# Retention attention with a gated linear unit: both weights through GpSimd's DMA queue, rounded to bfloat16 on the way

## The chip, the cores and the metric

The kernel runs on one core of a Trainium2 chip. The core has TensorE (PE; PEld is its weight load), VectorE (DVE), ScalarE (ACT) and GpSimd (POOL), which work at the same time on instructions of their own queues, each queue in its own order; SyncE (SP) does little but issue DMAs. ACT and POOL can issue DMAs too. Sixteen DMA engines move the data. The metric is the device time of one execution in microseconds (us); less is better.

## The reference

Inputs are float32: `q`, `k`, `v` of shape 8 x 8 x 576 x 64 (batch, heads, sequence, head width), two weights of 512 x 512 and the taps of a causal convolution, 5 x 512. The output is 8 x 576 x 512, float32.

```python
scores = (1 / np.sqrt(D)) * np.matmul(q, k.transpose(0, 1, 3, 2))
gamma = 1.0 - 2.0 ** (-5.0 - np.arange(H))
Dmat = np.where(rel >= 0, gamma[:, None, None] ** rel[None], 0.0)   # rel = query place - key place
x = np.matmul(scores * Dmat, v)          # 8 x 8 x 576 x 64, then heads side by side: 8 x 576 x 512
gate_pre = sum(conv_w[k] * xp[:, k:k + S, :] for k in range(5))   # xp: x with 4 zero rows ahead
gate = 1 / (1 + exp(-gate_pre))
out = (gate * (x @ w_val)) @ w_out
```

## The kernel before, in words

**Units.** The sequence of 576 is cut into units: for each of the 8 batches two full units of 256 rows, and two tail units, each with the last 64 rows of four batches. A unit's `q`, `k` and `v` are 512 KB each. The code counts units from 0; this text says first unit for unit 0. The work is pipelined over units: while one is multiplied, later ones are loaded, cast and transposed.

**Stages of a unit.** DMAs bring float32 tiles into slots `fk`, `fq`, `fv` (two slots each, of two halves; the first two units use larger slots, `big`, of which there are eleven). Casts make bfloat16 tiles `kb` and `qb` (L296, on POOL or ACT); `vb` is `v` times a decay, on POOL (L289). PE transposes `kb` and `qb` into PSUM, and ACT or DVE copies them to `kq`. PE makes scores from `kq`, DVE masks them into `p` (L385, L389). `update` multiplies keys by values, ACT copies the sum to `xf`, and POOL adds up the states carried along the sequence (`mid`, `run`, and their bfloat16 copies `s`, L520 to L531). `carried` and `values` make the attention's output in PSUM (`o`), DVE multiplies it by a decay into `xg` (L465). Then comes the gated unit: `conv` on PE and a sigmoid on ACT (`gate`, L576), `value` (`v<-xg,wvb`), the product of both on DVE (`z`, `zz`, L599), and `project` (`v<-wob,z`) with a copy to an output tile, which SP stores.

**What sets the order.** All of it is written out by hand, and each engine keeps the order in which its instructions are written. The first units are written one call after the other (L664 to L823), the others by a loop (L825). All matmuls are recorded at one line, L168.

**Loads and touches.** SP issues nearly all loads, in written order. A load waits until the slot's last reader is done. Where a load is given a `touch`, an engine first copies one element into the slot (L119), so that the DMA is issued only after that engine has come to this place in its own queue. A load can also be issued by ACT (`queue=nc.scalar`); it then stands in ACT's order. At most eight of these loads are under way: there are eight semaphores for them, used in turn, and each load waits for the landing of the one eight before it.

**The weights.** `w_val` and `w_out` are 1 MB each in float32. Both are loaded by SP in four DMAs of 256 KB. `w_val` (L150) goes through one slot of `fk` and one of `fq`, right behind the third unit's loads, and is cast to `wvb` by `prep_wv`: two casts on POOL (L265) and two on ACT (L267), which also swap the two halves of the partitions for `wvb[1]`. `w_out` (L160) goes through two slots of `big`, between the loads of the sixth and the seventh unit, and is cast to `wob` by `prep_wo` (L271), two casts on POOL, two on ACT. PE first needs `wvb` in `value(0, 0, 0)` (L755) and `wob` in the first `project` of the loop.

Of the kernel before, what the change touches and what calls it, by code (L numbers as in the profile page):

```python
# [13 lines left out]
F32 = mybir.dt.float32  # L14
# [7 lines left out]
def kernel(  # L22
# [29 lines left out]
    ldp = ctx.enter_context(tc.tile_pool(name="ld", bufs=2))  # L52
# [25 lines left out]
    half = (lo, hi)  # L78
    QUAD = ((0, 0), (1, 1), (0, 1), (1, 0))

    with tc.manual_schedule():
# [3 lines left out]
        def big():  # L85
            return ldp.tile([P, 2, DM], F32, name="big", bufs=11)
# [17 lines left out]
        def load_half(n, u, i, touch=None, queue=nc.sync):  # L104
            if u in whole:
                if i == 0:
                    load1(n, u, touch)
                return
            kind, b, c = units[u]
            if (n, u) not in loaded:  # L110
                t = ldp.tile([P, H, 2 * D], F32, name="f" + n)
                loaded[n, u] = [(t[:, g * HH:(g + 1) * HH], g * HH, HH) for g in range(2)]
                tiles[n, u] = t
            t = tiles[n, u]
            if kind == "tail" and i == 1:
                return
            hs = slice(i * HH, (i + 1) * HH)
            if touch:
                touch(t[0:1, i * HH, 0:1], lsc[0:1])  # L119
            if kind == "full":  # L120
                queue.dma_start(out=t[:, hs], in_=SRC[n][b, hs, c * W:(c + 1) * W, :].rearrange("h (p r) d -> p h (r d)", r=2))
            else:
                for g in range(GB):
                    nc.sync.dma_start(out=t[g * 32:(g + 1) * 32],
                                      in_=SRC[n][b + g, :, NC2 * W:S, :].rearrange("h (p r) d -> p h (r d)", r=2))

        def load(u):
            for n in "kqv":
                load1(n, u)
# [3 lines left out]
        cwn = consts.tile([KC * NP, 2, P], F32, name="cwn")  # L133
        taps = moe_conv_w.rearrange("k (o i) -> (k o) i", i=P)
        nc.scalar.dma_start(out=cwn, in_=taps.unsqueeze(1).to_broadcast([KC * NP, 2, P]))
        wvf = [None] * NP
        wvt = [None] * 2
        wof = [None] * NP
        load(1)


        def load_wv(o, touch=None):
            if wvf[o] is None:
                t = ldp.tile([P, 2, DM], F32, name=("fk", "fq")[o % 2])
                for i in range(2):
                    wvf[o % 2 + 2 * i] = t[:, i]
                wvt[o % 2] = t
            if touch:
                touch(wvf[o][0:1, 0:1], lsc[0:1])
            nc.sync.dma_start(out=wvf[o], in_=moe_w_val[o * P:(o + 1) * P, :])  # L150

        def load_wo(o, touch=None):
            if wof[o] is None:
                t = big()
                for c in range(2):
                    wof[o // 2 * 2 + c] = t[:, c]
            if touch:
                touch(wof[o][0:1, 0:1], lsc[0:1])
            blk = 2 * (o % 2) + o // 2
            nc.sync.dma_start(out=wof[o], in_=moe_w_out[blk * P:(blk + 1) * P, :])  # L160

        made = [0]
        BLOCK, PLACE = 127, 8
# [16 lines left out]
        lsc = small.tile([P, 1], F32, name="lsc")  # L180
# [64 lines left out]
        wvb = [consts.tile([P, 2, DM], BF16, name=f"wvb{e}") for e in range(2)]  # L245
        wob = consts.tile([P, NP, DM], BF16, name="wob")
        dg = consts.tile([P, NP, KC, 64], BF16, name="dg")

        def prep_conv():
# [9 lines left out]
                dg.rearrange("p o k j -> p k o j"),  # L259
                cw.rearrange("p (k o) -> p k o", o=NP).unsqueeze(3).to_broadcast([P, KC, NP, 64]),  # L260
                id2.unsqueeze(1).unsqueeze(1).to_broadcast([P, KC, NP, 64]), op=ALU.mult)

        def prep_wv():
            for i in range(2):
                nc.gpsimd.tensor_copy(wvb[0][:, i, :], wvt[0][:, i])  # L265
            for i in range(2):
                nc.scalar.copy(wvb[1][half[i]], wvt[1][half[1 - i]])  # L267

        def prep_wo(os, eng):
            for o in os:  # L270
                eng(wob[:, o, :], wof[o])  # L271

        def warm(n, cols=512, pool=None):
            z = (pool or ps_v).tile([P, 512], F32, name="s" if pool else "v")
# [24 lines left out]
        def cast1(n, u, eng=None):  # L299
            if u not in whole:  # L300
                for i in range(2):
                    cast_half(n, u, i, eng)
                return
            f = loaded[n, u][0][0]
            if n == "v":
                t = bfp.tile([P, H, 2, D], BF16, name="vb")
                nc.gpsimd.tensor_tensor(t.rearrange("p h r d -> p (h r) d"), f.rearrange("p h (r d) -> p (h r) d", r=2),
                                        gin[:, units[u][2]].rearrange("p h r -> p (h r)").unsqueeze(2)
                                        .to_broadcast([P, 2 * H, D]), op=ALU.mult)
            else:  # L310
# [344 lines left out]
        def gate_values(j, i, e):  # L655
            value(j, i, e)
            gated(j, i, e)

        table = small.tile([P, 1], F32, name="table")
        dve, act = nc.vector.tensor_copy, nc.scalar.copy  # L660

        pool = nc.gpsimd.tensor_copy
# [8 lines left out]
        prep_masks()  # L671
        cast1("v", 0)
        load(2)
        load_wv(0)
        load_wv(2)
        turn(0, ps_o, 0)
        take_part(0, 0, act)
        nc.scalar.activation(table, lsc, AF.Sigmoid)
# [23 lines left out]
        take_x(0, (1,))  # L702
        take_part(1, 1, dve)
        conv(0, 0)
        load_wv(1, act)
        load_wv(3)
        carried(1, 1, (0,))
        scores(1, 0)
        masks(1, 0)
        load_half("k", 3, 0, dve)  # L710
        scores(1, 1, pool=ps_a)
        masks(1, 1)
        load_half("k", 3, 1, dve)
        cast1("k", 2)
        update(1, own=True)
        cast1("q", 2, act)
        load_half("q", 3, 0, act)
# [18 lines left out]
        scores(2, 0)  # L736
        masks(2, 0)
        load_half("v", 3, 1, dve)
        prep_wv()
        cast1("k", 3)  # L740
        load_half("k", 4, 0)
        load_half("k", 4, 1)
# [8 lines left out]
        values(2, 1)  # L751
        take_x(2, (0,))
        load_half("v", 4, 0, dve)
        load_half("v", 4, 1)
        value(0, 0, 0)  # L755
        carried(2, 0)
        fence_last(2, dve)
# [2 lines left out]
        carried(2, 1)  # L760
        cast1("v", 3)
        cast1("q", 3, act)
        load_half("k", 5, 0, queue=nc.scalar)
        load_half("q", 5, 0, queue=nc.scalar)
        take_x(2, (1,))
        gated(0, 0, 1)
        load_half("k", 5, 1, dve)
# [11 lines left out]
        cast1("q", 4, act)  # L779
        conv(2, 0)  # L780
        cast1("v", 4)
        gate_values(1, 0, 1)
        load_wo(2, dve)
        load_wo(3)
        scores(3, 0)
        masks(3, 0)
        turn(4, ps_o, 0)
        take_part(4, 0, act)
        load_wo(0, dve)
        load_wo(1)  # L790
        turn(4, ps_o, 1)
        take_part(4, 1, act)
        scores(3, 1, pool=ps_a)
# [24 lines left out]
        load_half("k", 6, 1, dve)  # L818
        load_half("q", 6, 1)
        states(4, 1)  # L820
        prep_wo((0, 1), pool)
        cast_half("k", 6, 0)
        cast_half("q", 6, 0)  # L823

        for n in range(4, NU - 2):  # L825
            def bring(name, u, i, eng):
                if u < NU - 2:
                    load_half(name, u, i, eng)

            j, i = (HALVED, n - 4) if n < 6 else place[n - 2 - n % 2][0:1] + (n % 2,)  # L830
            rows = {4: [(0, 0), (0, 1), (1, 0)], 5: [(1, 1), (2, 0), (2, 1)]}.get(n, [(n - 3, 0), (n - 3, 1)])
            if NU - 2 <= n + 3 < NU:
                for name in "kqv":
                    load_half(name, n + 3, 0)
            scores(n, 1)
            masks(n, 1)
            conv(j, i)
            carried(n, 1)
            fence_last(n, dve)
            bring("k", n + 3, 0, act)  # L840
            scores(n + 1, 0, pool=ps_v)
            masks(n + 1, 0)
            update(n + 1, now=False)
            bring("q", n + 3, 0, act)
            if n == 4:
                prep_wo((2, 3), act)
            carried(n, 0)
            values(n, 0)
            values(n, 1)
            turns = ps_a.tile([P, 2, 2, 2, 2, P], BF16, name="a")  # L850
            turn_bank(n + 1, 1, turns[:, 0])
            gate_values(j, i, 0)
            bring("v", n + 3, 0, dve)
# [106 lines left out]
```

## Time and profile before

| | before |
|---|---|
| median of 3 runs | 156.38 us (155.78 to 156.86) |
| the profiled execution's own time | 157.37 us |
| its span, first to last instruction | 155.7 us |
| PE busy | 140.8 us (90%) |
| DVE, ACT, POOL busy | 105.7, 95.3, 102.0 us |
| DMA moved | 40.33 MB, 259 GB/s in the mean |
| PE in the chain that ended last | 69% |
| DMA in that chain | 13% |

The profile is of one execution. A row of a timeline gives the start in us from the first instruction, the time that the instructions of the row took, the engine, the line of the kernel, the operation, what it writes `<-` what it reads, the shape, and how many instructions the row stands for; in brackets the engine's idle time ahead of the row and what ended it. `SPq` and `ACTq` are DMA issues by SP and ACT. Buffer numbers are left out of the names, so that `fk` stands for either of its two slots and `s` for any of the bfloat16 states. Busy times overlap between engines, and matmuls are pipelined, so rows of PE overlap a little.

### The profile page before, as it was taken

The page shows a single profiled execution, that of the slowest core. Times are in us where ns is not written, and L with a number is a line of the kernel's source. Part 1 is how long each engine was busy: PE and PEld are TensorE (multiplying, and loading weights), DVE is VectorE, ACT ScalarE, POOL GpSimd, SP SyncE. Part 2 cuts the span into 40 slices and gives each one's busy share as a digit, 9 for nine tenths or more (in the row PEclk, how much of TensorE's full clock was granted, in tenths as well). Part 3 has the DMA queues.
Part 4 walks back from the last instruction along what each step waited for, and adds up shares of the span by engine and source line. Part 5 has one row for each costly group of instructions (what it writes and reads, how often), then busy time and mean ns, then how long its engine had stood idle before and what let it go on. Part 6 is the DMA issues. An engine that isn't in the chain of part 4 may idle for free.

```text
span 155.7 us, 7156 instructions
## 1 busy us (share of the span) xinstructions
PE 140.8 (90%) x3042; PEld 90.3 (58%) x3062; DVE 105.7 (68%) x222; ACT 95.3 (61%) x162; POOL 102.0 (66%) x167
## 2 busy tenths in 40 slices
PE   6877989969798999999999989999999999999960
PEld 2356667758557475656566555647565645457540
DVE  3877787558866567686968785876778687663130
ACT  6895756495576776756667675766665554533530
POOL 7578698649999949796978859797969334000000
PEclk9999999999999999999999999999999999999999
DMA  4999999989999887789887897999987899803355
GB/s 112 346 347 342 368 295 266 327 251 310 284 288 295 239 278 231 220 249 302 256 248 212 262 271 221 266 289 288 235 281 204 250 406 419 342 19 135 129 144 135
DMA packets 61042, 40.33 MB, mean 259 GB/s; under 512 B 2346, under 2 KB 57682, under 8 KB 61010
## 3 DMA queue, kind: packets, MB, share of 16 engines
q1 hardware_dynamic: 59808, 39.07, 81.7%
q10 hardware_dynamic: 1202, 0.81, 1.9%
q8 instruction: 24, 0.39, 1.0%
q14 instruction: 8, 0.07, 0.1%
HBM read 30.43 MB, written 9.44 MB: 256 GB/s over the span
## 4 chain that ended last, share of the span: by engine, by line
PE 69%; DMA 13%; DVE 7%; ACT 5%; issue 3%; SPq 0%; DVEq 0%; ACTq 0%
PE v L168 33%; PE a L168 19%; PE s L168 8%; PE o L168 8%; DMA fq<-in_q_dram 4%; DMA fq<-in_moe_w_val_dram 3%; ACT gate L576 3%; DMA fv<-in_v_dram 3%; DVE p L389 2%; DMA fk<-in_k_dram 2%; ACT wvb L267 1%; DMA cwn<-in_moe_conv_w_dram 1%; DVE dg L258 1%; DVE xg L465 1%; DVE kb L312 1%
## 5 line engine op out<-in xcount | busy, mean ns | idle before, releaser
L342 ACT COPY kq<-a 128x1024 bf16<-128x1024 bf16 x26 | 26.3, 1011 | 17.7 <-PE a L168 17.2
L289 POOL TENSOR_TENSOR vb<-fv,gin 128x512 bf16<-128x512 f32 x32 | 32.9, 1047 | 6.0 <-DMA fv<-in_v_dram 5.9
L168 PE MATMUL v<-xg,wvb 128*128 128x256 bf16 (+1 forms) x179 | 34.4, 322 | 0.7
L599 DVE TENSOR_TENSOR zz<-gate,v 128x512 bf16<-128x512 f32 x24 | 16.5, 688 | 15.0 <-PE v L168 12.4
L576 ACT ACTIVATE gate<-a 128x1024 f32<-128x1024 f32 (+1 forms) x17 | 16.6, 974 | 15.4 <-PE a L168 15.4
L389 DVE TENSOR_TENSOR p<-s,mask 128x1024 bf16<-128x1024 f32 x16 | 19.5, 1221 | 8.3 <-PE s L168 8.3
L168 PEld LDWEIGHTS <-wvb 128*128 128x128 bf16 x192 | 17.6, 98 | 11.4 <-issue 1.0
L465 DVE TENSOR_TENSOR xg<-o,gout 128x512 bf16<-128x512 f32 x32 | 22.3, 737 | 2.2 <-PE o L168 2.2
L296 POOL CAST kb<-fk 128x512 bf16<-128x512 f32 x32 | 19.5, 611 | 4.1 <-DMA fk<-in_k_dram 3.6
L168 PE MATMUL a<-xg,dg 64*64 64x256 bf16 (+1 forms) x460 | 21.7, 321 | 0.3 <-DVE xg L465 0.3
L168 PEld LDWEIGHTS <-kb 64*64 64x64 bf16 (+1 forms) x656 | 14.9, 106 | 8.7 <-DVE kb L312 1.0
L168 PE MATMUL v<-wob,zz 128*128 128x512 bf16 x82 | 19.7, 379 | 0.1
L614 ACT COPY big<-v 128x512 f32<-128x512 f32 x29 | 16.9, 581 | 4.2 <-PE v L168 3.7
L296 POOL CAST qb<-fq 128x512 bf16<-128x512 f32 x26 | 15.9, 613 | 2.1 <-DMA fq<-in_q_dram 1.2
L385 DVE TENSOR_TENSOR p<-v,mask 128x512 bf16<-128x512 f32 x26 | 16.7, 684 | 0.5
L168 PEld LDWEIGHTS <-kq 64*64 64x64 bf16 x576 | 11.3, 106 | 8.8 <-issue 7.6
L168 PEld LDWEIGHTS <-dg 64*64 64x64 bf16 x480 | 12.7, 106 | 4.9 <-issue 0.8
L168 PE MATMUL o<-p,vb 64*64 64x128 bf16 x576 | 13.3, 218 | 1.3 <-issue 0.4
L168 PEld LDWEIGHTS <-zz 128*128 128x128 bf16 x96 | 8.8, 98 | 8.9 <-DVE fv L119 0.5
L168 PEld LDWEIGHTS <-vb 64*64 64x64 bf16 x576 | 10.1, 107 | 2.9 <-issue 2.7
L168 PE MATMUL o<-kq,s 64*64 64x128 bf16 (+1 forms) x256 | 11.2, 212 | 0.2
L599 DVE TENSOR_TENSOR z<-gate,v 128x512 bf16<-128x512 f32 (+1 forms) x12 | 7.0, 589 | 5.6 <-PE v L168 5.5
(108 smaller groups left out, 209.1 us busy)
## 6 DMA issues: line engine op xcount, KB each, us to landing
out_dram<-big SPq DMA_DIRECT2D x16, 512.0 KB, 6.4
fv<-in_v_dram SPq DMA_DIRECT2D x28, 256.0 KB, 4.3
fk<-in_k_dram SPq DMA_DIRECT2D x27, 256.0 KB, 4.5
fq<-in_q_dram SPq DMA_DIRECT2D x27, 256.0 KB, 4.6
big<-in_k_dram SPq DMA_DIRECT2D x2, 512.0 KB, 4.9
big<-in_q_dram SPq DMA_DIRECT2D x2, 512.0 KB, 5.4
big<-in_v_dram SPq DMA_DIRECT2D x2, 512.0 KB, 5.9
big<-in_moe_w_out_dram SPq DMA_DIRECT2D x4, 256.0 KB, 5.0
```

The source lines that it names most:

```text
L168: return f(*a, **k)
L258: nc.vector.tensor_tensor(dg.rearrange("p o k j -> p k o j"), cw.rearrange("p (k o) -> p k o", o=NP).unsqueeze(3).to_broadcast([P, KC, NP, ...
L267: nc.scalar.copy(wvb[1][half[i]], wvt[1][half[1 - i]])
L289: nc.gpsimd.tensor_tensor(b[n][:, hs].rearrange("p h r d -> p (h r) d"), f.rearrange("p h (r d) -> p (h r) d", r=2), gin[:, units[u][2], h ...
L296: (eng or nc.gpsimd.tensor_copy)(b[n][:, :, hs].rearrange("p r h d -> p h r d"), f.rearrange("p h (r d) -> p h r d", r=2))
L342: (eng or nc.scalar.copy)(kqt[u][hf].rearrange("p i l r c a -> p (i l r c a)"), ps.rearrange("p i l r a -> p (i l r a)"))
L385: nc.vector.tensor_tensor(p[:, par].rearrange("p l r a -> p l (r a)"), sps[u, hf][par].rearrange("p l r a -> p l (r a)"), mrow.to_broadcas ...
L389: nc.vector.tensor_tensor(p.rearrange("p e l r a -> p (e l) (r a)"), sps[u, hf].rearrange("p e l r a -> p (e l) (r a)"), mrow.to_broadcast ...
L465: nc.vector.tensor_tensor(x[:, b, :, PAD + i0:PAD + i0 + P].rearrange("p o (a r) -> p o r a", r=2), o[c].rearrange("p o (r a) -> p o r a", ...
L576: nc.scalar.activation(t, cps[j, i], AF.Sigmoid)
L599: nc.vector.tensor_tensor(zsb[j][:, 2 * e + ss[0]:2 * e + ss[-1] + 1, :], gsb[j, i][e], vps[j, i, e], op=ALU.mult)
L614: (eng or nc.scalar.copy)(outs[u][:, r], o)
```

## The change

Three things change. First, both weights are loaded by DMAs that POOL issues and that write bfloat16 straight into `wvb` and `wob`: three DMAs for `w_val` (one of 128 partitions, two of 64, which swap the halves), two for `w_out`. The float32 slots, the touches and all eight casts of weights go. The three stand on POOL right behind the third unit's `kb` casts and ahead of the second unit's state sums (`mid`, `s`); the two stand behind the fifth unit's `vb` and ahead of the sixth unit's `kb`. Second, the fourth unit's keys are loaded where the weights were, right behind the third unit, and without touches. Third, the first halves of the sixth unit's keys and queries go from ACT's queue to SP's, behind the first half of the fifth unit's values, whose second half goes from SP's queue to ACT's.

```diff
-        def load_wv(o, touch=None):
-...
-            nc.sync.dma_start(out=wvf[o], in_=moe_w_val[o * P:(o + 1) * P, :])
-        def load_wo(o, touch=None):
-...
-            nc.sync.dma_start(out=wof[o], in_=moe_w_out[blk * P:(blk + 1) * P, :])
+        def load_wv():
+            src = moe_w_val.rearrange("(i e p) n -> e p i n", e=2, p=P)
+            nc.gpsimd.dma_start(out=wvb[0], in_=src[0])
+            for i in range(2):
+                nc.gpsimd.dma_start(out=wvb[1][half[i]], in_=src[1][half[1 - i]])
+
+        def load_wo():
+            src = moe_w_out.rearrange("(b a p) n -> a p b n", b=2, p=P)
+            for a in range(2):
+                nc.gpsimd.dma_start(out=wob[:, 2 * a:2 * a + 2, :], in_=src[a])
...
-        def prep_wv():
-            for i in range(2):
-                nc.gpsimd.tensor_copy(wvb[0][:, i, :], wvt[0][:, i])
-            for i in range(2):
-                nc.scalar.copy(wvb[1][half[i]], wvt[1][half[1 - i]])
-
-        def prep_wo(os, eng):
-            for o in os:
-                eng(wob[:, o, :], wof[o])
...
         load(2)
-        load_wv(0)
-        load_wv(2)
+        load_half("k", 3, 0)
+        load_half("k", 3, 1)
...
         conv(0, 0)
-        load_wv(1, act)
-        load_wv(3)
         carried(1, 1, (0,))
         scores(1, 0)
         masks(1, 0)
-        load_half("k", 3, 0, dve)
         scores(1, 1, pool=ps_a)
         masks(1, 1)
-        load_half("k", 3, 1, dve)
         cast1("k", 2)
+        load_wv()
         update(1, own=True)
...
         load_half("v", 3, 1, dve)
-        prep_wv()
         cast1("k", 3)
...
         load_half("v", 4, 0, dve)
-        load_half("v", 4, 1)
         value(0, 0, 0)
...
         cast1("q", 3, act)
-        load_half("k", 5, 0, queue=nc.scalar)
-        load_half("q", 5, 0, queue=nc.scalar)
+        load_half("v", 4, 1, queue=nc.scalar)
+        load_half("k", 5, 0)
+        load_half("q", 5, 0)
...
         cast1("v", 4)
+        load_wo()
         gate_values(1, 0, 1)
-        load_wo(2, dve)
-        load_wo(3)
...
-        load_wo(0, dve)
-        load_wo(1)
...
         states(4, 1)
-        prep_wo((0, 1), pool)
         cast_half("k", 6, 0)
         cast_half("q", 6, 0)
...
-            if n == 4:
-                prep_wo((2, 3), act)
             carried(n, 0)
```

More of the change, by code (lines that the diff above doesn't have):

```diff
@@ L135 @@
         nc.scalar.dma_start(out=cwn, in_=taps.unsqueeze(1).to_broadcast([KC * NP, 2, P]))
-        wvf = [None] * NP
-        wvt = [None] * 2
-        wof = [None] * NP
         load(1)
-        def load_wv(o, touch=None):
-            if wvf[o] is None:
-                t = ldp.tile([P, 2, DM], F32, name=("fk", "fq")[o % 2])
-                for i in range(2):
[L146 to L150, printed above, removed]
-        def load_wo(o, touch=None):
[L153 to L159, printed above, removed]
-            nc.sync.dma_start(out=wof[o], in_=moe_w_out[blk * P:(blk + 1) * P, :])
+        def load_wv():
[7 more added lines that the diff above has]
+                nc.gpsimd.dma_start(out=wob[:, 2 * a:2 * a + 2, :], in_=src[a])
         made = [0]
@@ L261, in prep_conv @@
                 id2.unsqueeze(1).unsqueeze(1).to_broadcast([P, KC, NP, 64]), op=ALU.mult)
-        def prep_wv():
-            for i in range(2):
-                nc.gpsimd.tensor_copy(wvb[0][:, i, :], wvt[0][:, i])
-            for i in range(2):
-                nc.scalar.copy(wvb[1][half[i]], wvt[1][half[1 - i]])
-        def prep_wo(os, eng):
-            for o in os:
-                eng(wob[:, o, :], wof[o])
         def warm(n, cols=512, pool=None):
```

## The prediction

> **What bounds the kernel now.** I read the page first, then the PE timeline with its idle times, then ACT, POOL and the queues where PE waits.
>
> From the page, and from the PE timeline between 10 and 54 us (start, duration, engine, instructions, in brackets the idle time before and its releaser):
>
> ```profile
> PE 140.8 (90%) x3042; PEld 90.3 (58%) x3062; DVE 105.7 (68%) x222; ACT 95.3 (61%) x162; POOL 102.0 (66%) x167
> ```
> ```profile
> 18.20 0.30 PE L168 MATMUL o<-kq,s 64*64 64x128 bf16 x4
> ...
> 30.49 0.62 PE L168 MATMUL o<-ident,kb 128*128 128x128 bf16 x8
> 31.75 0.40 PE L168 MATMUL o<-ident,qb 128*128 128x128 bf16 x4 [0.64 <-ACT qb L296]
> 32.43 0.40 PE L168 MATMUL o<-ident,qb 128*128 128x128 bf16 x4 [0.29 <-ACT qb L296]
> 33.35 0.42 PE L168 MATMUL a<-kq 64*64 64x128 bf16 x16 [0.52 <-ACT gate L576]
> ...
> 36.80 0.40 PE L168 MATMUL a<-ident,kb 128*128 128x128 bf16 x4
> 37.12 0.40 PE L168 MATMUL a<-ident,qb 128*128 128x128 bf16 x4
> ```
>
> PE sets the time. In the chain that ended last, the score matmuls of the loop recur at 54.57, 61.71, 68.85, 75.98, 83.12 us: 7.14 us a unit, with gaps of 0.05 us. From 54 us on nothing but PE work counts, and the change leaves its matmuls alone. So the question is how much sooner or later PE reaches 54 us. Its visible gaps from 14 to 54 us come to some 5 us; those at 39 to 41 us are released by DVE's masks, which the change doesn't touch. The three rows at 31.75 to 33.35 are the ones that it can reach. What they wait for, on ACT and in the SP queue:
>
> ```profile
> 31.07 1.30 ACT L296 CAST qb<-fq 128x512 bf16<-128x512 f32 x2 [2.16 <-DMA fq<-in_q_dram]
> 32.28 1.02 ACT L576 ACTIVATE gate<-a 128x1024 f32<-128x1024 f32 x1
> ```
> ```profile
> 13.13 2.39 SPq L150 DMA_DIRECT2D fk<-in_moe_w_val_dram  x2
> 15.70 0.80 SPq L150 DMA_DIRECT2D fq<-in_moe_w_val_dram  x2
> 16.60 1.20 SPq L121 DMA_DIRECT2D fk<-in_k_dram  x2
> ...
> 24.39 1.01 SPq L121 DMA_DIRECT2D fq<-in_q_dram  x2
> ```
>
> The fifth unit's queries (24.39) land at 31.05 and 31.73; the casts and the gate queue behind them on ACT. The reader should also see POOL, where the new DMAs go:
>
> ```profile
> 15.09 0.61 POOL L296 CAST kb<-fk 128x512 bf16<-128x512 f32 x1 [0.33 <-DMA fk<-in_k_dram]
> 16.86 0.73 POOL L520 TENSOR_TENSOR mid<-run,xf 128x256 f32<-128x256 f32 x1 [1.15 <-ACT xf L497]
> 17.65 0.40 POOL L521 CAST s<-mid 128x256 bf16<-128x256 f32 x1
> ...
> 20.68 1.16 POOL L265 CAST wvb<-fk 128x512 bf16<-128x512 f32 x2
> ...
> 33.35 2.04 POOL L289 TENSOR_TENSOR vb<-fv,gin 128x512 bf16<-128x512 f32 x2 [2.90 <-DMA fv<-in_v_dram]
> 35.34 1.16 POOL L296 CAST kb<-fk 128x512 bf16<-128x512 f32 x2
> 36.45 1.17 POOL L296 CAST qb<-fq 128x512 bf16<-128x512 f32 x2
> ```
>
> POOL is idle for 1.15 us before `mid`, and its `s`, done at 18.05, is used by PE at 18.20: no slack.
>
> **Part 1, the stall at 31 us goes.** Without the stall the two groups of eight transposes need 0.92 us from 30.49 (four take 0.23 us where nothing holds them, 49.73 to 49.97), so L168 `a<-kq` starts at 31.41 instead of 33.35: **-1.94 us**. Does the data come in time? In the changed order SP issues the fourth unit's keys at 13.13 and 15.09 in the weights' places; values and queries still wait for their touches, so the order from there is paced by DVE and ACT. The fifth unit's keys follow DVE's touch at 21.58, and its queries need a slot that ACT's casts free at 18.1, not at 23.2 after the `wvb` casts: they go at about 22.7 and 23.2 rather than 24.39 and 24.90. The two halves on ACT's queue that shared the engines with them (24.25, 25.84; 0.5 MB, 1.4 us at the 0.72 us per 256 KB at which loads land in a row) move behind the fifth unit's values. With 4.5 us to land, the median of its kind, the queries are there at 27.2 to 28 us, before ACT is free at 28.9. Casts end at 30.05, the gate at 31.07. The values land by 30 rather than 33.2 and 33.9, so POOL's 2.90 us goes too. What is late next is PE itself. ACT's one issue in place of two (0.47 and 0.37) falls into its idle 1.54 us before 27.35. The sixth unit's keys and queries, now on SP behind a touch at 24.06 and one at 27.17, follow in the row of landings to 33 or 34, before POOL's casts want them (part 3).
>
> ACT loses 2.1 us of `wvb` casts and 1.1 of `wob`, POOL 1.16 and 1.17, DVE four touches of 0.13 and ACT one. I cost these at nothing: they lie beside PE's matmuls, and PE waits for none of them but through the queries, counted above; if that cover were gone, the 2.1 us would be the gain. SP's eight issues count only through the order above.
>
> **Part 2, three DMAs ahead of `mid` on POOL.** The weight transfers stand right behind the cast at 15.09, whose end is 15.70, and POOL runs in order. With d us for one issue, `mid` starts at 15.70 + 3d instead of 16.86. Behind it are `s`, the second `s` and the third unit's `vb`; PE waits for the first. Taking 0.1 us of slack, PE is late by **S = 3d - 1.26** (nothing below d = 0.42). From 18.3 to 31.1 PE has 0.44 us of gaps, so S stays, and touches, loads and casts that hang on PE move with it. POOL itself has caught up by the 1.16 us of the `wvb` casts, so no second delay arises.
>
> **Part 3, two DMAs ahead of `kb` on POOL.** They follow the fifth unit's `vb`. Freed from the DMA wait, POOL's chain there hangs on `xf` (ACT, ends 28.91 + S): `mid` and `s` 1.19, `vb` 2.04, the issues 2d, `kb` 1.11, the first `qb` 0.61: 33.9 + S + 2d. PE would like that `qb` at 37.03 - 1.94 + S = 35.1 + S. So PE is late by **2d - 1.2** more. In the kernel before, the 2.90 us in which POOL waited would have covered the issues; it is gone with the stall of part 1. The `wob` casts fall out later (41.29), when DVE and PE set the pace, so they give nothing back. The transfers have eight us until L168 `v<-wob,z` at 43.90.
>
> **The size of d.** No DMA is issued by POOL before. From below: a 256 KB load takes SP or ACT 0.33 to 0.47 us to issue when nothing holds it. From above: POOL's longest instruction here, 1.90 us. On POOL the cores must do the work in software, so I take the row of a simple POOL instruction over a tile, 0.61 us, and that of a two-operand one, 1.04, and their middle, **d = 0.8**. Sum: S 1.14 - 1.94 + 0.40 = **-0.4 us**. The profiled execution took 157.37 us (span 155.7 and 1.67 around it) and would come to 157.0; it lies 0.99 above the median of the runs, 156.38, from which I forecast **156.0 us**.
>
> The Trainium skill, page DMA: Bandwidth & Descriptors, section on the anatomy of a DMA on the gpsimd path, says that descriptor generation is small and that many descriptors can be emitted before their cost shows; no run here shows it yet. By it d would be near the lower row and the sum -1.9. The same page of the Trainium skill gives, in its Specifications, about 1 us to the first byte on that path; by it, an estimate, d = 1 and the sum +0.6.
>
> **Rivals.**
> A, issues nearly free: d at 0.4 to 0.55. For it speaks that SP's issues are 0.4 with more descriptors. Sum -1.94 to -1.55: **154.4 to 154.8**.
> B, POOL becomes the bound, the other side: at d = 0.9 the sum is nil, from there each 0.1 us of d costs 0.5 us. At d = 1.2: S 2.34 - 1.94 + 1.2 = +1.6, **158.0**; at 1.5: +3.1, 159.5. For it: there are 256 runs of 2 KB in a whole transfer, and `s` has no slack. Against: POOL's other instructions of this size are near 0.6. The Trainium skill, page SBUF — State Buffer, section on the two sides, says that GpSimd can't write descriptors while VectorE makes a two-port copy; the only SBUF-to-SBUF copies near here are touches of 0.13 us, so by it B would grow by two or three tenths.
> C, transfers that round are slower than plain ones. The 1 MB of value weights took 3.15 us of landings (17.97 to 21.12). PE needs them at 23.31 + S = 24.45; starting near 17.5 they may take 2.2 times as long for nothing. At four times they land near 30.1: +5.6, in all **161**. From below, nothing is to be gained by fewer bytes written, as nothing waits for the weights. The trace has no such transfer; DMA engines 90% busy up to 50 us speak for some harm.
> D, the change doesn't bring the loads forward: the same bytes pass before the fifth unit's values, and they land at 33.9 as before. Then the old stall stays and hides S, but the two issues stand between `vb` and `kb` uncovered: 2d less the 0.1 us by which PE waited at 37.12 anyway, +1.5: **157.9**. Against it: 0.5 MB of the sixth unit no longer passes first, and the queries are issued 1.7 us sooner.
>
> **From cases to numbers.** Forecast (d 0.6 to 1.1) 0.43, A 0.23, B 0.21, D 0.06, C 0.07. A change under 1% (1.56 us) can't be told from none here. Faster by over 1%: A, 0.24 with a little of the forecast's edge. Slower by over 1%: B, C and most of D, 0.33. Same: 0.43. The range takes in A's 154.4 and B up to d = 1.35 (+2.3): **154.2 to 158.7**; d near 1.9 (+5) and C lie outside.
>
> **What would show it.** POOL's idle row before `mid` gone and `mid` at 15.7 + 3d; L168 `o<-kq,s` at 18.2 + S; ACT's 2.16 us before the `qb` casts and POOL's 2.90 before `vb` gone; PE's wait before the first `qb` of the sixth unit (`a<-ident,qb`) 2d - 1.2; from the fifth unit on 7.14 us a unit as before. The prediction is wrong if PE waits for `wvb` or `wob` themselves, if the first POOL DMA costs far more than the next, or if the clock, full in every slice now, drops after a longer gap at 18 us.

## Result, and the profile after

The changed kernel takes 157.92 us (157.02 to 160.39, six runs) against 156.22 us for the kernel before beside it (154.81 to 157.75, six runs). The ratio is 1.0106, with a 95% interval from 1.0065 to 1.0147: slower by 1.1%, or **+1.7 us**, where -0.4 us was forecast. Timed again twice on other occasions it gave 157.59 and 157.88, with ratios of 1.0080 [1.0038, 1.0121] and 1.0101 [1.0048, 1.0155]. Medians here are over all runs, ratios leave out those that the chip disturbed.

The first profiled execution of the changed kernel, 160.39 us, holds three waits of PE for POOL's casts, 1.34, 0.16 and 0.40 us, at 122 to 127 us, that no other profile of it has at that size, so the lines below are from a later profile of the same kernel (157.92 us, span 156.2). Of the three profiles of the changed kernel it is the only one whose first scores come as early as in the kernel before. It is set beside a later profile of the kernel before as well (155.74 us, span 154.0): the execution from which the prediction was worked, 157.37 us, turned out not to be a usual one, as the second experiment shows.

PE's timeline, changed kernel (start, duration, engine, line, operation, in brackets the idle time ahead and what ended it):

```profile
18.99 0.30 PE L156 MATMUL o<-kq,s 64*64 64x128 bf16 x4 [0.65 <-POOL s L499]
...
32.41 0.40 PE L156 MATMUL o<-ident,qb 128*128 128x128 bf16 x4 [0.31 <-ACT qb L274]
33.33 0.42 PE L156 MATMUL a<-kq 64*64 64x128 bf16 x16 [0.52 <-ACT gate L554]
...
36.78 0.40 PE L156 MATMUL a<-ident,kb 128*128 128x128 bf16 x4
37.87 0.40 PE L156 MATMUL a<-ident,qb 128*128 128x128 bf16 x4 [0.69 <-POOL qb L274]
```

L156 is the line of all matmuls here, L168 before. The later profile of the kernel before has neither the first wait nor the last:

```profile
18.19 0.30 PE L168 MATMUL o<-kq,s 64*64 64x128 bf16 x4
...
36.16 0.39 PE L168 MATMUL a<-ident,qb 128*128 128x128 bf16 x4
```

`o<-kq,s` waits for POOL as forecast; the wait before the scores at 33.33 is still there; and there is a new wait before the sixth unit's `qb`. POOL's timeline, changed kernel:

```profile
15.61 0.90 POOL L141 DMA_DIRECT2D wvb<-in_moe_w_val_dram  x1
16.50 1.22 POOL L143 DMA_DIRECT2D wvb<-in_moe_w_val_dram  x2
17.71 0.76 POOL L498 TENSOR_TENSOR mid<-run,xf 128x256 f32<-128x256 f32 x1
...
32.61 2.04 POOL L267 TENSOR_TENSOR vb<-fv,gin 128x512 bf16<-128x512 f32 x2 [1.66 <-DMA fv<-in_v_dram]
34.59 1.49 POOL L148 DMA_DIRECT2D wob<-in_moe_w_out_dram  x2
36.08 1.18 POOL L274 CAST kb<-fk 128x512 bf16<-128x512 f32 x2
```

The issues take 0.90, 0.61, 0.61 and 0.75, 0.75 us: 2.12 and 1.49, a mean of 0.72. ACT's timeline shows when the fifth unit's queries came:

```profile
30.80 0.62 ACT L274 CAST qb<-fq 128x512 bf16<-128x512 f32 x1 [1.12 <-DMA fq<-in_q_dram]
31.74 0.62 ACT L274 CAST qb<-fq 128x512 bf16<-128x512 f32 x1 [0.32 <-DMA fq<-in_q_dram]
```

ACT still waits for them, till 30.80 and 31.74; forecast was 27.2 to 28. In the later profile of the kernel before, the same casts start at 29.60 and 30.88:

```profile
29.60 0.62 ACT L296 CAST qb<-fq 128x512 bf16<-128x512 f32 x1 [0.28 <-DMA fq<-in_q_dram]
30.88 0.62 ACT L296 CAST qb<-fq 128x512 bf16<-128x512 f32 x1 [0.66 <-DMA fq<-in_q_dram]
```

Where the time goes, by the start of the same matmuls in these two profiles (us):

| matmuls | before | changed | later by |
|---|---|---|---|
| first scores | 8.21 | 8.23 | 0.02 |
| scores behind the second unit's `o<-kq,s` | 19.65 | 20.52 | 0.87 |
| scores ahead of the fifth unit's transposes | 30.55 | 30.91 | 0.36 |
| scores behind `gate` | 32.48 | 33.33 | 0.85 |
| `v<-kq` behind the sixth unit's `qb` | 36.88 | 38.60 | 1.72 |
| scores on entering the loop | 53.15 | 54.86 | 1.71 |
| `v<-kq` seven units on | 104.66 | 106.27 | 1.61 |

So 0.85 us is lost at 18 us, the kernel is again as far behind at 33, 0.87 is lost at 37, and the loop hardly gives any of it back. The fall to 0.36 at 31 us is this profile's of the kernel before: from the scores at 19.65 to those at 30.55 it takes 0.42 us longer than the first one (19.66 to 30.14). The late queries then put the changed kernel back to 0.85. At the end this pair differs by more than 1.7: the spans are 154.0 and 156.2. The changed kernel waits once more in the tail units, where no profile of the kernel before waits for POOL:

```profile
124.89 0.40 PE L156 MATMUL a<-ident,qb 128*128 128x128 bf16 x4 [0.55 <-POOL qb L274]
```

One of its two other profiles has no such wait, and what brings it about was not followed up. So the two places explain 1.7 us of this pair's 2.2; that they equal the difference of the medians is in part chance.

### The profile page after: what moved, and what is told of

Its sections match the earlier page's. It is cut to its first block, busy times and chain, and to the rows that moved or that the text cites. A ratio compares the mean times of both kernels' runs of the same rounds, so it can differ in the third digit from the quotient of the medians.

```text
span 158.7 us, 7155 instructions
## 1 busy us (share of the span) xinstructions
PE 142.4 (90%) x3062; PEld 90.7 (57%) x3062; DVE 105.8 (67%) x218; ACT 92.0 (58%) x157; POOL 103.7 (65%) x168
## 3 DMA queue, kind: packets, MB, share of 16 engines
q0 software_dynamic: 1104, 1.05, 4.6%
## 4 chain that ended last, share of the span: by engine, by line
PE 60%; POOL 10%; DMA 10%; SPq 6%; DVE 4%; issue 4%; ACT 3%; DVEq 0%; POOLq 0%
PE v L156 31%; PE a L156 15%; PE s L156 8%; PE o L156 7%; DMA fq<-in_q_dram 5%; SPq L124 4%; DMA fv<-in_v_dram 4%; SPq L121 2%; DVE p L367 2%; POOL kb L274 2%; POOL vb L267 2%; POOL qb L274 2%; DMA cwn<-in_moe_conv_w_dram 2%; POOL vb L285 1%; ACT L656 1%
## 5 line engine op out<-in xcount | busy, mean ns | idle before, releaser
L156 PE MATMUL v<-xg,wvb 128*128 128x256 bf16 (+1 forms) x192 | 35.2, 326 | 0.4 <-issue 0.4
L156 PEld LDWEIGHTS <-wvb 128*128 128x128 bf16 x192 | 17.6, 97 | 11.9 <-issue 1.6
L156 PE MATMUL a<-xg,dg 64*64 64x256 bf16 (+1 forms) x460 | 21.7, 321 | 0.3 <-DVE xg L443 0.3
L156 PEld LDWEIGHTS <-kb 64*64 64x64 bf16 (+1 forms) x656 | 15.3, 107 | 9.5 <-POOL kb L274 1.5
L156 PE MATMUL v<-wob,zz 128*128 128x512 bf16 x84 | 19.9, 379 | 0.0
L156 PEld LDWEIGHTS <-kq 64*64 64x64 bf16 x576 | 11.4, 106 | 10.2 <-issue 9.3
L156 PEld LDWEIGHTS <-dg 64*64 64x64 bf16 x480 | 12.7, 106 | 4.8 <-issue 0.9
L156 PEld LDWEIGHTS <-zz 128*128 128x128 bf16 x96 | 8.8, 98 | 8.9 <-DVE fv L119 0.5
L156 PE MATMUL o<-p,vb 64*64 64x128 bf16 x576 | 13.0, 218 | 0.5 <-DVE p L367 0.4
L477 ACT COPY xf<-s 128x512 f32<-128x512 f32 x14 | 8.1, 579 | 6.6 <-PE s L156 6.5
L156 PE MATMUL o<-kq,s 64*64 64x128 bf16 (+1 forms) x256 | 11.0, 212 | 0.5 <-POOL s L499 0.5
L156 PE MATMUL a<-ident,kb 128*128 128x128 bf16 x104 | 10.2, 220 | 1.3 <-POOL kb L274 1.3
```

The source lines that it names most:

```text
L156: return f(*a, **k)
L477: nc.scalar.copy(xf.rearrange("p c o d -> p c (o d)"), xyt[:, :, 0:NP * 64])
```

## Experiments

**1. The changed kernel again.** Theory P: the issue times on POOL are the cost. Theory F: PE's instruction fetch is held up while rounding transfers move, because the first profile had gaps of 1.05 and 0.42 us inside groups of matmuls at 21 to 27 us.

> The changed kernel once more, nothing left out, for a second profile. In the first one PE stood still for 1.05 us at 21.35 and 0.42 us at 26.36 in the middle of a group of matmuls, waiting for nothing that the profile shows, and the tail units' loads came 1.8 us late from 107 us on. Theory F (PE's instruction fetch is held up while the rounding transfers move): the stalls near 21 and 26 us come back, the ones after 107 us don't. Theory P (only the issue times on POOL count): the stalls are chance and gone, while the waits for POOL at 18.7 (0.5 us) and 37.7 us (0.6) come back. Time against the kernel before by both: 1.01.

> The changed kernel on the same chip as the three others, as their yardstick: 157.5 to 158.0 by every theory, first scores later than 8.4 us by theory Q, anywhere from 8.2 on by theory C.

157.59 and 157.88 us. Neither profile has the gaps inside groups at 21 to 27 us, and the time is the same: F falls. Gaps of this kind, with no releaser in the trace, occur in the kernel before too (0.50 us at 20.25 in the later profile). Of the waits for POOL that P expected, the one before the sixth unit's `qb` is in both (0.67 and 0.69 us), the one for `s` only in the second (0.65); in the other profile the first scores come as late as 9.52, and PE doesn't wait for `s`.

**2. The kernel before again, for its profile.**

> The kernel before, unchanged, for a second profile. Theory B (the base of the sum): the profiled execution that the prediction was worked from took 157.4 us where the median of many is 155.9, so its stall at 31 us, or a hiccup later, is longer than usual, and part 1 was credited with a gain that most executions don't have to give. B expects a shorter stall before the scores at 33 us here (PE waits there of under 1 us where 1.45 were shown) or an earlier first score. Theory P (only the issue time on POOL matters) expects the same stall, with a span of 154 to 155 us reached some other way.

> The kernel before once more, for a third profile: B expects the stall at 31 us to differ from profile to profile by more than 0.5 us; P expects it within 0.2 us of the first profile's.

155.83 and 155.74 us. The scores behind `gate`, in PE's timeline of these two:

```profile
32.24 0.42 PE L168 MATMUL a<-kq 64*64 64x128 bf16 x16 [0.51 <-ACT gate L576]
```
```profile
32.48 0.42 PE L168 MATMUL a<-kq 64*64 64x128 bf16 x16 [0.51 <-ACT gate L576]
```

Both waits of PE before the transposes of `qb`, 0.64 and 0.29 us in the first profile, are gone, and the scores start at 32.24 and 32.48, not 33.35, from first scores within 0.1 us of each other. Theory B holds: the stall varies from one execution to the next. Of four profiles with the old loads (the fourth is that of experiment 9), two have the long one and took 157.4 and 157.2 us; the two with the short one took 155.8, near the median. Part 1 was credited with a stall that, by these times, the median execution doesn't have; some 0.65 us was there to win, not 1.94: in these two profiles the transposes begin at 30.67 and 30.90, and by the prediction's 0.92 us for them the scores could have begun at 31.59 and 31.82.

**3. One weight at a time.** With `w_val` alone through POOL, the change's order of loads is kept and `w_out` goes back to SP; with `w_out` alone, all else is as before:

```diff
         cast1("v", 4)
-        load_wo()
         gate_values(1, 0, 1)
+        load_wo(2, dve)
+        load_wo(3)
...
```

> The changed kernel with w_out as before (SP, float32 slots, casts); w_val alone goes by POOL. P: the wait for POOL near 37.7 us (0.6 us) is gone, that at 18.7 stays: 0.6 us below the changed kernel, about +1.0 us against before. F: the stall near 21 us stays; what w_out costs is then its own share of the loss, and the time lies between before and the changed kernel.

> The kernel before with w_out alone by POOL, rounded on the way; w_val and all other loads as before. P: the two issues (1.5 us) stand uncovered between vb and kb, since the fifth unit's values land as late as before: +1.4 us. F: as P, and a stall of PE near 39 to 41 us, while the transfers move, comes on top. If neither holds, no difference.

`w_val` alone: 156.83 us, ratio 1.0075 [1.0043, 1.0107]. `w_out` alone: 157.85, ratio 1.0117 [1.0075, 1.0160], as dear as the whole change. In its profile POOL issues from 34.52 to 36.13 and PE waits 0.25 us for `kb` and 0.70 for `qb`: two issues in a busy stretch of POOL stand uncovered. The two prices, 0.9 and 1.9, add up to more than the change's 1.7; why was not followed up.

**4. The order of loads alone**, the weights as before:

> The kernel before, with only the order of loads changed: the second half of the fifth unit's values on ACT's queue, the first halves of the sixth unit's keys and queries on SP's behind them; weights loaded and cast as before. Rival D (the loads come no sooner for it): 155.9, the same within 0.5 us. If the order brings the fifth unit's values and queries forward by the 1.4 us that the prediction gave it: POOL's wait for the values shorter by 1 us or more, the time 0.3 to 0.8 us less. If the order itself harms: 156.5 or more.

156.37 us, ratio 0.9991 [0.9953, 1.0029]: no change. In its profile the wait before the scores is gone (32.04, no idle time), 0.44 us under the later profile of before; the time doesn't resolve that. So with SP's plain weights the order does a little good. What the change loses is not in it.

**5. The issues moved.** Three behind `s` and two behind the sixth unit's `qb`; then, in another kernel, only the two for `w_out`, ahead of the fifth unit's `vb`, where POOL waits:

```diff
         cast1("k", 2)
-        load_wv()
         update(1, own=True)
+        load_wv()
```
```diff
+        load_wo()
         cast1("v", 4)
-        load_wo()
```

> The changed kernel with POOL's five issues moved behind what PE waits for: the three behind mid and both s, the two behind the sixth unit's qb casts. P: PE's waits at 18.7 (0.5 us) and 37.7 us (0.6) are gone: 1.1 us below the changed kernel, close to before or 0.5 us faster. F: the stalls in the middle of groups only move with the transfers, about 2 us later, and most of the loss stays: within 0.5 us of the changed kernel.

> The changed kernel, with the two issues for w_out moved ahead of the fifth unit's vb, where POOL waits 1.2 to 1.4 us for its values. Theory P (the issues cost what POOL's order exposes): PE's wait before the sixth unit's kb and qb, 0.6 to 0.8 us, falls to 0.2 or less; time 0.5 to 0.8 us under the changed kernel's 157.6 to 157.9, so 156.9 to 157.3. Theory T (the transfers of the weights hold up the loads): no better than the changed kernel, 157.6 or more, because w_out would then share the engines with the sixth unit's loads.

Behind `s`: 161.38 us, ratio 1.0340 [1.0298, 1.0381], which neither P nor F had expected. The first issue ends at 19.63 and its data lands at 24.52; PE waits 0.84 and 2.07 us for `wvb` itself, and from 27.1 to 30.5 us the granted clock is 0.50. With 4.9 us and more from the end of an issue to landing there is no room to issue later.

Ahead of `vb`: 158.39 us, ratio 1.0098 [1.0056, 1.0140], no gain. The profiled execution is the slowest of the twelve, 161.0 us. In it PE's wait for the sixth unit's `qb` is gone, as P said, and by 39 us this kernel is only 0.7 us behind the later profile of before, where the changed kernel is 1.7. Then, in PE's timeline:

```profile
41.03 0.32 PE L156 MATMUL s<-vb,kb 64*64 64x64 bf16 x16 [1.14 <-POOL vb L267]
43.77 0.43 PE L156 MATMUL s<-vb,kb 64*64 64x64 bf16 x16 [2.42 <-POOL vb L267]
```

and in POOL's:

```profile
39.94 1.04 POOL L267 TENSOR_TENSOR vb<-fv,gin 128x512 bf16<-128x512 f32 x1 [2.01 <-DMA fv<-in_v_dram]
42.67 1.04 POOL L267 TENSOR_TENSOR vb<-fv,gin 128x512 bf16<-128x512 f32 x1 [1.69 <-DMA fv<-in_v_dram]
```

The sixth unit's values, issued at 31.50 and 32.18, just beside the two POOL DMAs (31.55 and 32.31), take 8.3 and 10.4 us to land; in the changed kernel they take 4.5 and 4.6. The granted clock is then 0.50 from 41.6 to 48.4 us. In this execution theory T (the transfers of the weights hold up the other loads) has its case: transfers side by side, and the one that PE needs first is late. The single runs of this kernel lie from 156.7 to 161.0, so it doesn't always end like this, and why the median is no better than the changed kernel's is not shown.

**6. `w_out` in POOL's wait, `w_val` on SP**, with the order of the change:

> w_val as in the kernel before, the order of the fifth and sixth units' loads as in the changed one, and w_out by two POOL DMAs ahead of the fifth unit's vb, in POOL's wait for the values. Theory P (an issue in POOL's idle time costs nothing): 155.5 to 156.1, no slower than the kernel before, 1.5 to 2 us under the kernel with w_out behind vb (157.85). Theory T (the rounding transfers themselves harm): 156.6 or more.

157.53 us (155.86 to 160.75), ratio 1.0053 [1.0013, 1.0093]. That lies where T had it (156.6 or more) and not P (155.5 to 156.1). Its profile, at 156.07, near the fastest of the twelve, has no wait for the issues and enters the loop 0.46 us behind the later profile of before, 0.45 of which it lost ahead of the first scores. P's mechanism holds in that execution; the kernel does not beat the one before, and what delays its other runs was not seen.

**7. Issues without bytes, the weights loaded as before.** The five DMAs stand at the change's places and write 32 bytes a row into a small tile that nothing reads; in the second kernel this tile has 512 bytes a partition and not 384:

```diff
-        tiny = consts.tile([P, 12, 16], BF16, name="tiny")
+        tiny = consts.tile([P, 16, 16], BF16, name="tiny")
```

> The kernel before, with its weights as before, and five DMAs more on POOL at the two places of the change, each with as many rows as the real one but 16 elements of a row instead of 512 (32 bytes written): the issue time without the transfer. Theory P (issue time on POOL is the cost): PE waits for s at 18.2 us by 0.5 to 1 us, most of it lost again in the stall at 31 us, and for the sixth unit's kb and qb by 0.5 to 1 us; time 156.4 to 157.9, like the kernel with w_out alone on POOL's queue (157.85). Theory T (the rounding transfers hold up the other loads): 156.2 or less, because the bytes are missing.

> As the kernel with the five short DMAs, with one change: the small tile that they write takes 512 bytes of a partition and not 384. In the first try all loads were slower from 5 us on (290 KB per us where others moved 346), long before POOL issued anything, so that its time, 162.1, can't be laid to the issues. Theory A (the 384 bytes had shifted every later tile off its 512-byte grid): loads at 346 KB per us again and a time 4 to 6 us less. Theory Q (a POOL queue with short rows slows the DMA engines by being there): 290 KB per us again, 162. If A holds, theory P expects 156.8 to 158 (issue time on POOL alone does the harm), theory T (the transfer's bytes do it) 156.3 or less.

162.07 us, ratio 1.0375 [1.0331, 1.0419], and 158.73 us, ratio 1.0156 [1.0097, 1.0216]. The table by stretches (us of the stretch, busy time of PE, PEld, DVE, ACT, POOL, granted clock, DMA share, GB/s) of the first and of the second, long before POOL issues anything:

```profile
5.00:15.00 10.00, 7.87 (x172) 5.11 (x174) 7.57 (x15) 7.39 (x13) 5.31 (x7) 1.00 1.20 291
```
```profile
5.00:15.00 10.00, 9.23 (x174) 6.17 (x176) 7.54 (x15) 7.38 (x13) 6.62 (x8) 1.00 1.15 345
```

The later profile of the kernel before moves 345 in this stretch. The two kernels differ in the size of this tile alone, so its 384 bytes made the loads slower, as theory A has it; that the place of the later tiles is the reason is argued. With 512 bytes the kernel still takes 2.5 us more than the one before, and T's 156.3 or less is out; it lies above P's 156.8 to 158 as well. The 2.5 us are not the issues alone: in its profile the first scores come 0.94 us late, PE waits 0.75 us at 32 us for nothing that the profile shows and 0.69 for the queries, and 0.56 and 0.71 for POOL's `kb` and `qb` behind the two issues. An issue takes as long with rows of 32 bytes as with rows of 1 KB: 0.90 and 1.22 us for the first three, 1.49 for the two, as above.

**8. Without touches.** SP issues the fourth unit's queries and values as soon as their slots allow:

```diff
-        load_half("q", 3, 0, act)
+        load_half("q", 3, 0)
```

and so for the other three halves.

> The changed kernel without the touches on the fourth unit's queries and values, so that SP issues them as soon as their slots allow. Theory L (the fifth unit's queries come no sooner because SP's order from 18 us on is paced by touches that hang on PE, and the engines move a quarter less while they wait): fifth unit's queries landed by 29 to 30 instead of 32.1, the wait before the scores at 33 us gone, 0.4 to 0.6 us less than the changed kernel: 157.1 to 157.4. Rival: the loads then share the engines with the rounding transfers, wvb lands after 24 us and PE waits for it: 158.5 or more.

157.49 us, ratio 1.0075 [1.0039, 1.0111], the changed kernel's time. Theory L is right in part about the loads. SP comes to the fifth unit's queries 2.0 and 0.4 us sooner:

```profile
22.82 2.79 SPq L121 DMA_DIRECT2D fq<-in_q_dram  x2
```

The first of the two issues takes 2.05 us and ends at 24.87, only 0.4 us sooner than in the changed kernel. The queries land at 29.48 and 30.21, not 30.78 and 31.72, which is still 2.2 us behind the prediction's 27.2 to 28. The waits before the scores at 33 us and before the sixth unit's `qb` are gone. The rival is right as well. PE's timeline:

```profile
25.18 0.92 PE L156 MATMUL v<-xg,wvb 128*128 128x256 bf16 x7 [0.50 <-DMA wvb<-in_moe_w_val_dram]
```

`wvb` lands at 25.05, since the loads now share the engines with it. That, two gaps without a releaser (0.55 and 0.64 us), the late `s` and, in this profile, a start 0.55 us late make up for what was won.

**9. Does a POOL queue delay the start?** One short POOL DMA in the kernel before, late in the loop:

> The kernel before, with one short DMA more on POOL (256 rows of 32 bytes written, into a tile of 512 bytes a partition that nothing reads), put in the loop at the tenth unit, where POOL waits 1.0 to 1.4 us for ACT. Seen so far: in eight of ten profiles of kernels with a POOL queue the first scores start 0.2 to 1.3 us later than 8.2 us, in none of four without. Theory Q (a POOL queue delays the start by being in the program): first scores later than 8.4 us, time 156.5 or more. Theory C (the late starts are chance): first scores by 8.3, 155.8 to 156.3, as the kernel before.

156.04 us, ratio 1.0007 [0.9968, 1.0047], first scores at 8.25: theory C. One short POOL DMA late in the program costs nothing; what several early ones do to the start it doesn't tell. Its profile has the long stall of the first profile of before, once more:

```profile
32.21 0.40 PE L170 MATMUL o<-ident,qb 128*128 128x128 bf16 x4 [0.71 <-ACT qb L298]
33.08 0.40 PE L170 MATMUL o<-ident,qb 128*128 128x128 bf16 x4 [0.47 <-ACT qb L298]
34.00 0.42 PE L170 MATMUL a<-kq 64*64 64x128 bf16 x16 [0.52 <-ACT gate L578]
```

**10. No weights, and issues without bytes, in the changed order.** `wvb` and `wob` are filled with a constant by DVE; then the five issues come back with rows of 32 bytes:

```diff
+        for e in range(2):
+            nc.vector.memset(wvb[e], 0.03)
...
+        nc.vector.memset(wob, 0.03)
...
-        load_wv()
...
-        load_wo()
```

> The changed kernel without any transfer of weights: wvb and wob are filled with a constant by VectorE early, in its idle time, so the output is that of constant weights. It has the change's order of loads without its issues and without the 2 MB. If part 1 is right that the order brings the loads forward once the weights are out of the way: no wait at 18, 25, 33 or 37 us, loop entry 1 to 2 us sooner than in the kernel before, 154.0 to 155.2. If the touches alone set the loads' times, 155.5 to 156.3.

> As the kernel without weights, but with the change's five POOL issues at their places, each row of 32 bytes and not 1 KB: the issue time without the bytes. Against the kernel without weights it tells the issues' price, against the changed kernel the price of the bytes. Theory P (issue time on POOL is most of the loss): 1.2 to 1.8 us above the kernel without weights, within 0.6 us of the changed kernel, 156.8 to 157.8. Theory T (the bytes are most): within 0.5 us of the kernel without weights, 1 us or more under the changed kernel.

156.69 us, ratio 1.0050 [1.0017, 1.0082], and 158.12 us, ratio 1.0104 [1.0044, 1.0165]. Both profiles bear some 0.8 us of the filling itself (PE waits 0.78 us for DVE at 17 us), which hides the late `s`; so they are compared with each other. Issues: 158.12 - 156.69 = **1.43 us**, without the late `s`; by the ratios 0.8, with intervals that overlap. Bytes: the changed kernel beside them took 157.88, which is 0.24 less than without bytes: **not to be told from nothing**, if the filling's 0.78 us here is set against the 0.87 that the late `s` costs there. And without any weights the queries still come late. By stretches, changed kernel without weights:

```profile
18.00:24.00 6.00, 5.31 (x166) 3.89 (x165) 5.11 (x12) 2.21 (x7) 4.23 (x7) 1.00 0.45 127
```

and ACT's timeline of the same:

```profile
30.91 1.27 ACT L265 CAST qb<-fq 128x512 bf16<-128x512 f32 x2 [0.84 <-DMA fq<-in_q_dram]
```

The DMA engines are half idle from 18 to 24 us (share 0.45, where the kernel before has 1.05), and ACT waits for the queries till 30.91 all the same. The expectation of 154.0 to 155.2 fails. The 156.69 lie above the other range too (155.5 to 156.3), by less than the filling. SP issues the queries at 24.82 and 25.36, as in the changed kernel (24.78 and 25.32), so neither the weights' bytes nor POOL's issues set when these loads go; SP's order does, of which the touches are a part (experiment 8).

## Why the prediction was wrong, point by point

**Part 2 was right.** d was taken as 0.8 us and is 0.71 for these three issues. By S = 3d - 1.26 that makes 0.86 us; measured are 0.85 (0.87 less the 0.02 at the start). POOL's idle row before `mid` is gone and `mid` starts at 17.71, where 15.61 + 2.12 is 17.73. By the scores at 30.91 S was still 0.77 us against the first profile of the kernel before, and 0.36 against the later one. The size holds for an early start only: in the two other profiles of the changed kernel, whose first scores are 0.47 and 1.31 us late, only 0.64 and 0.18 us more have been lost by the scores behind `o<-kq,s`.

**Part 1 failed: the term -1.94 measured 0.** It failed twice over. First its size: the stall of the one profile was taken for the usual one (experiment 2). Then its mechanism, the step "the queries are there at 27.2 to 28 us". SP was to issue them at about 22.7 and 23.2 us. It issued them at 24.78 and 25.32, a little later than before (24.38 and 24.89), and they landed 1.2 and 0.9 us later. SP's timeline, changed kernel and then the later profile of the kernel before:

```profile
18.26 1.68 SPq L121 DMA_DIRECT2D fq<-in_q_dram  x2
21.41 1.55 SPq L121 DMA_DIRECT2D fv<-in_v_dram  x2
23.06 1.67 SPq L121 DMA_DIRECT2D fk<-in_k_dram  x2
24.78 1.05 SPq L121 DMA_DIRECT2D fq<-in_q_dram  x2
```
```profile
24.38 1.01 SPq L121 DMA_DIRECT2D fq<-in_q_dram  x2
```

The 4.5 us to land, a median, failed as well: these two took 6.0 and 6.4 us, and some 6.1 even without any weights under way (experiment 10). In the profile from which the prediction was worked the same two loads, issued at 24.39 and 24.90, had taken 6.7 and 6.8. In SP's order they stand behind the fourth unit's queries and values, which wait for touches, at 19.6, 21.4 and 22.6 us, and behind the fifth unit's keys; those touches hang on DVE and ACT and move with S, as the prediction itself says of touches. That the slot came free 5 us sooner was worth nothing behind them (experiment 10); with those touches gone the queries landed 1.3 and 1.5 us sooner, not the 3.6 that were missing (experiment 8), and what held back the rest is not shown. The prediction also left out a load: ACT's queue issues 256 KB of the fifth unit's values at 24.87 us, between the two halves of the queries, in the place of the 256 KB of the sixth unit's keys that it had counted as gone.

**Part 3 was right in mechanism and undersized by what part 1 left.** 2d - 1.2 with the measured d of 0.75 is 0.3; measured are 0.87. The 1.2 came from freeing POOL of its wait for the values. But `vb` starts at 32.61, not at 31 or so, because the values land no sooner either; behind it the two issues of 1.49 us stand in front of `kb` and `qb`.

With its own formulas, the measured d and nothing from part 1 the sum would have been +0.86 + 0.3 = +1.2, and with part 3 as measured in this one profile it is +1.7.

**The rivals.** D came true, the case with a chance of 0.06: loads no sooner, the two issues uncovered, 157.9. Its mechanism holds with one correction: the queries come later by about S (1.2 and 0.9 us), so the old stall hides nothing of it in the end, and the issues cost 0.87 and not 1.5. That the two come to the same sum, and so to 157.9, is luck. The "against" it was given, that 0.5 MB less goes first and the queries are issued 1.7 us sooner, was the same unproved step. A (issues nearly free) falls with d at 0.72. B's border was right only with part 1's gain in the sum. C falls: `wvb` has landed by 23.24 us in the changed kernel and PE needs it at 24.17, and experiment 10 finds no price for the rounding and its bytes where they stand. They do cost where they meet a load that PE waits for (experiment 5).

On the Trainium skill, page DMA: Bandwidth & Descriptors, section Anatomy of one DMA — SWDGE (gpsimd) path, which calls descriptor generation small: here an issue held POOL for 0.61 us with 128 rows and 0.73 to 0.90 with 256, whatever the row's length. By the page the sum would have been near -1.9; the measurement decides.

**What stays open.** In seven of the ten profiles whose kernels have POOL DMAs near 18 or 35 us (leaving out the first kernel of experiment 7 and those of 10, whose starts have other causes) the first scores come 0.2 to 1.3 us late; in all five others (experiments 2, 4 and 9, and the first profile of before) they come by 8.3 us. Full clock is first granted at 4.5 to 6.6 us in the profiles with an early start and at 7.2 to 9.3 in those with a late one. The Trainium skill, page TensorE: Matmul & The Clock Gate, section What's actually happening, says that the clock's window runs freely and doesn't begin with the kernel; by it this would be chance, and the last profile of the changed kernel, at 8.23, fits that. But if seven late starts fell on these fifteen profiles by chance alone, all five others would be spared in only 56 of 3003 ways (an estimate from these counts). So it is not excluded that the POOL DMAs delay the start. That the last profile loses 1.7 us by the loop with a start at 8.23 shows that the start isn't needed to explain the result; in the two profiles with a late start, the start and the late `s` together make 1.1 and 1.5 us, and they enter the loop 2.1 us behind.

## What to carry to other kernels

A load comes sooner only if the instruction that issues it does: follow the queue's order through every wait ahead of it, the touches too, and the loads that are under way beside it, before a freed slot or freed bandwidth is counted. A DMA issued by GpSimd costs GpSimd its issue time, 0.6 to 0.9 us here, so it belongs where GpSimd waits anyway, and its transfer where no urgent load lands. A stall that is to be removed should be seen in more than one profile, above all when the profiled run is slower than the median.

## What had not been expected of the hardware

- **A small tile ahead of the others slowed the loads.** With a tile of 384 bytes a partition ahead of the others the loads moved 291 GB/s, with 512 bytes 345 (experiment 7); the medians differ by 3.3 us.
- **The clock can halve soon after a wait of one us.** In the profile of `w_val` alone PE waits 1.01 us for `s` at 18.2 us, and the table by stretches then shows the granted clock (0.51):

```profile
21.50:25.00 3.50, 3.35 (x104) 3.35 (x103) 2.51 (x6) 0.52 (x2) 1.47 (x3) 0.51 0.94 268
```

It halved in both kernels of experiment 5 too, at waits of 0.84 to 2.42 us. But the changed kernel's wait of 0.65 us had no such consequence, nor had two waits of 0.92 and 1.24 us in the first kernel of experiment 7 (clock 1.00 from 17 to 30 us), and most runs with `w_val` alone show a clock of 0.99 or more. So the wait alone doesn't decide it, and the limit was not found.
- **Rounding on the way saves the engines nothing.** A packet that reads 2 KB and writes 1 KB took 98 ns in the median, a plain one of 2 KB 84 ns; the POOL queue's 1.05 MB took 4.5% of the engines' 156.2 us, 7.0 us in all.
